# One tile for the last 64 query rows of both heads of a pair, in causal attention ahead of two MLPs

## The chip, the cores and the metric

The kernel runs on one core of a Trainium2 chip. The metric is the device time of one execution in microseconds (us). Five engines work side by side, each through its own queue in order: PE (TensorE, matrix products; PEld are its weight loads), DVE (VectorE), ACT (ScalarE), POOL (GpSimd) and SP (which only issues DMAs).

## What is computed

The reference, cut to what matters (B = 2 batches, H = 8 heads, S = 576 positions, D = 64):

```python
scores = q @ k.T / sqrt(D)                       # per batch and head, 576 x 576
bias = -(cum[:, None] - cum[None, :])            # cum: running sum of max(s, 0)
scores = where(causal, -1e9, scores + minimum(bias, 0))
attn = softmax(scores)                           # each query row over its keys
x = (attn @ v) -> [1152 tokens, 512]
x = leaky_relu(x @ w_in) @ w_out                 # d_ff 2048
out = sum over 4 experts e of p[:, e] * (relu(x @ w1[e]) @ w2[e])   # F 1024
```

576 is four and a half tiles of 128 query rows. All is float32; the two weights of the first MLP arrive as 64-bit floats and are converted on the chip.

## The kernel before

**Attention.** The work is cut into 16 units. A unit is one batch, one pair of heads and one part of the query rows: units 0 to 7 take rows 0 to 255 (tiles 0 and 1), units 8 to 15 rows 256 to 575 (tiles 2, 3 and 4). Tile 4 has only 64 rows left, so it is laid over rows 448 to 575 (`tiles` holds `min(i * P, S - P)`): its first 64 rows are tile 3's last once more, and what is computed for them is overwritten. A unit of the second kind has six items, tile 4, 3, 2 for head 0 and 1 each: (4,0), (4,1), (3,0), (3,1), (2,0), (2,1).

Each item goes through steps that lag behind each other, by the table `STEPS`: in iteration i of the loop the program writes the scores of item i, the exponentials of item i-1, the transposes of item i-3, the products with values of item i-5 and `finish` of item i-7.

- `scores`: in a unit of the second kind, q and k are split into a high and a low part; two products (`ks,qs` and `kd,qs`) go into the PSUM tile `ps_sc`. One DVE instruction (shown as CUSTOM_DVE_ANT_0) adds the mask, scales, writes `z` and keeps the row's minimum `mn`. Tile 4 has 576 keys and goes in two pieces, 448 and 128.
- `exps`: ACT turns `z` into the exponentials.
- `transposes`: PE turns each 128 x 128 block of `z` (five for tile 4) into `ps_pt`, ACT copies that to `pv`.
- `values`: PE multiplies each block of `pv` (the stationary operand) with 65 columns of `vs` (a column of ones for the row sums, and 64 of v) into `ps_o`. These are plain float32 products: each stands as two instructions, so tile 4 shows as x10 for one head. After the last item of a unit DVE divides (`st`, `xo`).
- `finish`: three transposes of `xo` into `ps_x`, and one ACT copy to `x`.

**What is woven in.** Between the steps, at two of the three `yield`s of an iteration, the program advances `main`, the first MLP for the first 512 tokens (`ps_u`, `ps_d`: three or so 512-column products a step). `WOVEN * KD / (2.0 * (48 - 6))` sets how many steps per `yield`: 72 over 84, 0.857. At two of three it also advances `units_of_w` (`supply`: the conversion of the 64-bit weights, 16 blocks `r`, mostly DVE work of 1024 columns into `raw`, which then go to DRAM as `w_f`) and `late` (weight blocks loaded back from `w_f`). `split_keys` prepares the keys and queries of the next unit (`qs`, `ks`) in four calls, one per iteration, from the unit's first item on; the last DVE operation of it, the second `ks<-kr,ks`, stands in the fourth item's iteration.

Up to the end of the attention every engine keeps the order in which the program is written (`keep_in_program_order`). The loop's first part ends at iteration 39; while there is little of `main` to weave, it puts small products on `idle` there. When the attention is done, DVE and POOL prepare the second half of the first MLP (`t`, `sums`, `w`), which PE begins when the first half's `ps_d` are done. The queues of DMAs: SP issues the loads of q, k, v (`qr`, `kr`, `vs`) and the loads from `w_f`, POOL the load `kd<-in_k_dram`, ACT the 64-bit weights.

Of the kernel before, what the change touches and what calls it, by code (L numbers as in the profile page):

```python
# [19 lines left out]
def attention_moe_moe2(ctx: ExitStack, tc: tile.TileContext, q, k, v, s, w_in, w_out, probs, w1, w2, out):  # L20
# [34 lines left out]
    P = 128  # L55
# [469 lines left out]
    mask = ap.tile([P, S], F32, name="mask", bufs=1)  # L525

# [53 lines left out]
    q_s = [ap.tile([P, 2, 2, S // 2 + 32], F32R, tag=f"q{i}", name="qs", bufs=1) for i in range(2)]  # L580
    q_e, k_e = [], []

    def pads(pool):
# [15 lines left out]
        ones = pool.tile([P, 2, S // 2 + 32], F32, name="ones")  # L599
        nc.gpsimd.memset(ones[D:DK], 1.0)  # L600
        return ones
# [10 lines left out]
    def load_keys(n, queue=None):  # L612
# [9 lines left out]
        else:  # L622
            qr = ap.tile([P, 2, S // 2 + 32], F32, tag="qr", name="qr")
            for j in range(2):
                nc.sync.dma_start(qr[j * D : (j + 1) * D], q_of)
# [14 lines left out]
    def split_keys(n):  # L640
# [7 lines left out]
        nc.scalar.copy(qs[:, 0], qr)  # L648
        yield
        nc.vector.tensor_tensor(qs[:D, 1], qr[:D], f32(qs[:D, 0]), ALU.subtract)  # L650
# [16 lines left out]
    class Unit:  # L667
# [3 lines left out]
        def __init__(self, n):  # L671
            b, hp, i0, i1 = self.of = of_unit(n)
            self.items = [(i, j) for i in reversed(range(i0, i1)) for j in range(2)]
# [5 lines left out]
        def scores(self, i, j):  # L679
# [6 lines left out]
            own = slice(a - tiles[i0][0], kw - tiles[i0][0])  # L686
            for pc, keys in enumerate([slice(0, kw)] if kw <= 512 else [slice(0, a), slice(a, kw)]):
# [6 lines left out]
                nc.vector.tensor_tensor_reduce(  # L694
                    out=z[:, keys], in0=ps, in1=mask[:, S - kw + keys.start : S - kw + keys.stop], scale=-(D ** -0.5),
# [18 lines left out]
        def values(self, i, j):  # L714
# [3 lines left out]
            pv, cols = self.pv.pop((i, j)), slice(j * (D + 1), (j + 1) * (D + 1))  # L718
# [11 lines left out]
        def finish(self, i, j):  # L730
# [5 lines left out]
            base, q0, q1 = tiles[i0][:2] + tiles[i1 - 1][2:]  # L736
            x = ps_t.tile([P, 512], F32, tag="pt", name="ps_x")[:, : q1 - base]
            for i in reversed(range(i0, i1)):
                nc.tensor.transpose(x[:, tiles[i][0] - base : tiles[i][2] - base], self.xo[:, i - i0].rearrange("p h c -> p (h c)"), ident)
# [5 lines left out]
            else:  # L745
                nc.scalar.copy(x_t[1][:, hp, dst], x)
# [187 lines left out]
```

## Time and profile before

| | |
|---|---|
| median of 3 timed runs | 726.08 us (724.13, 726.08, 728.84) |
| span of the profiled execution | 724.3 us, first to last instruction; no other time of that execution is given |
| PE busy | 708.1 us, 98% of the span |
| DVE, ACT, POOL busy | 442.5, 322.8, 253.1 us |
| units 8 to 15 (first score to the end of the last transposes) | 51.8 to about 209 us |

The profiled execution lies within the three timed ones. In the rows below nearly every instruction stands on line 43, since one helper issues them all; they are told apart by the tile names. A matmul row's time is from its start to its modelled end, and those overlap: what a chain of products costs is read from the start of its first to the start of what follows it on PE.

### The profile page before, as it was taken

Reading aid. Unit: us, or ns where it says so; the run is one execution under the profiler, and the core shown is the slowest. Engines: PE = TensorE matmul, PEld = TensorE weight load, DVE = VectorE, ACT = ScalarE, POOL = GpSimd, SP = SyncE. Lnnn points to the kernel's source line nnn. Section 1 sums busy time; section 2 is a strip of 40 time slices with the busy share of each in tenths; the row PEclk is TensorE's granted clock in tenths of the full one; section 3 lists DMA queues with packets and bytes.
Section 4 is the critical chain, followed back from the end, with each engine's and each line's share of the span. In section 5 each row is a group of like instructions: output and inputs, shape, how many; then the busy total and the mean of one; then the engine's idle time right before and its main releaser. Section 6 shows DMA issues by size and latency. Waiting matters only on the chain.

```text
span 724.3 us, 11414 instructions
## 1 busy us (share of the span) xinstructions
PE 708.1 (98%) x4376; PEld 645.2 (89%) x4376; DVE 442.5 (61%) x901; ACT 322.8 (45%) x650; POOL 253.1 (35%) x226
## 2 busy tenths in 40 slices
PE   7889999999999999999999999999999999999998
PEld 7779889888878999999988989989889898898996
DVE  5878797998769656844953644545436354364452
ACT  4767877876645755534432322314224133232220
POOL 5000000000018788883362442704625227142200
PEclk9999999999999999999999999999999999999999
DMA  8876867585452232221120202102102011020002
GB/s 217 228 194 176 217 181 240 184 246 181 176 203 88 76 99 89 63 84 59 33 85 1 88 29 59 59 1 59 58 30 59 30 60 59 0 59 1 1 30 101
DMA packets 41878, 70.68 MB, mean 98 GB/s; under 512 B 4112, under 2 KB 23328, under 8 KB 41824
## 3 DMA queue, kind: packets, MB, share of 16 engines
q1 hardware_dynamic: 31296, 41.87, 20.0%
q10 hardware_dynamic: 9376, 25.73, 10.9%
q0 software_dynamic: 1152, 2.36, 1.6%
q8 instruction: 34, 0.56, 0.3%
q14 instruction: 20, 0.16, 0.1%
HBM read 59.11 MB, written 10.82 MB: 97 GB/s over the span
## 4 chain that ended last, share of the span: by engine, by line
PE 89%; DMA 3%; DVE 3%; ACT 2%; issue 1%; POOL 1%; ACTq 0%; DVEq 0%; POOLq 0%; SPq 0%
PE ps_d L43 40%; PE ps_u L43 36%; PE ps_o L43 5%; PE ps_sc L43 4%; PE ps_pt L43 3%; DMA raw<-w_f 1%; DMA cum_d<-cum 1%; DMA ke<-cum 1%; DVE t L43 1%; ACT z L43 1%; ACT w L43 1%; DVE w L43 0%; ACT pv L43 0%; DVE z L43 0%; DMA w_f<-raw 0%
## 5 line engine op out<-in xcount | busy, mean ns | idle before, releaser
L43 PE MATMUL ps_u<-t,w 128*128 128x320 f32 (+1 forms) x1680 | 236.5, 299 | 1.2 <-DVE t L43 1.2
L43 PEld LDWEIGHTS ps_u<-t,w 128*128 128x128 f32 x1680 | 233.0, 189 | 4.8 <-DVE t L43 1.4
L43 PE MATMUL ps_d<-w,ht 128*128 128x512 f32 (+1 forms) x876 | 203.4, 388 | 0.0
L43 PEld LDWEIGHTS ps_d<-w,ht 128*128 128x128 f32 x876 | 161.0, 188 | 31.5
L43 POOL TENSOR_TENSOR w<-raw,w 128x512 fp32r<-128x512 f32 (+2 forms) x72 | 108.5, 1527 | 219.1 <-ACT w L43 219.1
L43 ACT ACTIVATE ht<-ps_u 128x320 fp32r<-128x320 f32 (+2 forms) x176 | 74.3, 433 | 161.6 <-DVE ps_u L43 129.1
L43 DVE SCALAR_TENSOR_TENSOR oacc<-ps_d,pn,oacc 128x512 f32<-128x512 f32 (+1 forms) x64 | 47.5, 743 | 104.0 <-PE ps_d L43 104.0
L43 PE MATMUL ps_d<-ht,w 128*128 128x320 f32 (+1 forms) x576 | 109.6, 340 | 1.0 <-DVE y L43 1.0
L43 ACT CAST w<-raw 128x512 fp32r<-128x512 f32 (+2 forms) x96 | 64.6, 710 | 82.5 <-PE ps_d L43 76.0
L43 PEld LDWEIGHTS ps_d<-ht,w 128*128 128x128 f32 x576 | 90.9, 188 | 7.0 <-ACT t L43 1.4
L43 DVE SCALAR_TENSOR_TENSOR ht<-ps_u,ht 128x320 fp32r<-128x320 f32 (+1 forms) x128 | 56.4, 453 | 23.3 <-ACT ht L43 22.0
L43 PEld LDWEIGHTS ps_o<-vs,pv 128*128 128x128 f32 x480 | 63.0, 191 | 8.5 <-issue 4.0
L43 DVE TENSOR_TENSOR ps_u<-ps_u,tmp 128x320 f32<-128x320 f32 (+1 forms) x120 | 56.2, 471 | 23.3 <-PE ps_u L43 21.7
L43 PE MATMUL ps_o<-vs,pv 128*128 128x65 f32 x480 | 62.9, 267 | 2.9 <-issue 1.3
L43 DVE TENSOR_TENSOR tmp<-ps_u,tmp 128x320 f32<-128x320 f32 (+1 forms) x80 | 36.9, 464 | 40.2 <-PE ps_u L43 39.3
L43 POOL TENSOR_TENSOR w<-sums,w 128x1024 fp32r<-128x1024 f32 x24 | 58.6, 2443 | 7.5 <-ACT w L43 7.5
L43 POOL TENSOR_TENSOR sums<-raw 128x256 f32<-128x256 f32 x48 | 38.1, 812 | 59.3 <-DMA raw<-w_f 57.8
L43 PE MATMUL ps_u<-x,w 128*128 128x512 f32 x192 | 56.7, 411 | 0.9 <-DVE x L43 0.9
L43 ACT ACTIVATE z<-z,mn 128x256 f32<-128x256 f32 (+4 forms) x80 | 48.5, 607 | 20.2 <-DVE mn L43 16.7
L43 POOL DMA_DIRECT2D kd<-in_k_dram x8 | 5.1, 639 | 141.4 <-PE ps_sc L43 141.4
L43 DVE CUSTOM_DVE_ANT_0 z<-ps_sc,mask 128x256 f32<-128x256 f32 (+4 forms) x80 | 41.0, 513 | 15.4 <-PE ps_sc L43 13.8
L43 ACT COPY pv<-ps_pt 128x512 f32<-128x512 f32 (+3 forms) x96 | 38.9, 422 | 13.0 <-PE ps_pt L43 12.4
(77 smaller groups left out, 659.2 us busy)
## 6 DMA issues: line engine op xcount, KB each, us to landing
raw<-in_moe_w_dram SPq DMA_DIRECT2D x32, 512.0 KB, 3.6
raw<-w_f SPq DMA_DIRECT2D x24, 512.0 KB, 4.0
r<-in_moe_w_in_dram ACTq DMA_DIRECT2D x8, 1024.0 KB, 6.6
w_f<-raw ACTq DMA_DIRECT2D x16, 512.0 KB, 4.1
r<-in_moe_w_out_dram ACTq DMA_DIRECT2D x8, 1024.0 KB, 7.9
qr<-in_q_dram SPq DMA_DIRECT2D x16, 160.0 KB, 7.3
kd<-in_k_dram POOLq DMA_DIRECT2D x8, 288.0 KB, 7.5
kr<-in_k_dram SPq DMA_DIRECT2D x8, 288.0 KB, 3.7
```

Source lines behind the costliest of these rows:

```text
L43: ins = call(*args, **kw)
```

## The change

The 64 last rows of the two heads of a pair become one tile of 128 rows, head 0 in rows 0 to 63, head 1 in rows 64 to 127. Its item is (4, None); a unit of the second kind has five items in place of six, 72 instead of 80 in all. For the scores, `qs` gets 64 columns of zeros and head 1's last 64 rows are put ahead of its others, so that a window of 128 columns holds [last rows of head 0, zeros] and another [zeros, last rows of head 1]; four products (two of each head) are summed in one `ps_sc`. A mask of its own, `mask2`, serves the last 128 keys. There is then one minimum, one exponential, one set of five transposes, and the products with values take both heads' 130 columns at once. `finish` copies the result in three pieces. `qr` is loaded in six DMAs in place of two. The weaving's numbers are set to 40 items in place of 48, and `units_of_w` gets one more step in every third iteration.

```diff
+    mask2 = ap.tile([P, P], F32, name="mask2", bufs=1)
...
+    LAST = S - (QT - 1) * P
+    QC = S - half[0]
+    q_s = [ap.tile([P, 2, 2, QC + LAST], F32R, tag=f"q{i}", name="qs", bufs=1) for i in range(2)]
...
+        for x in q_s:
+            nc.gpsimd.memset(f32(x[:, :, 0, QC:]), 0.0)
+        own = mask2[:, P - LAST :]
+        nc.gpsimd.memset(mask2, 0.0)
+        nc.gpsimd.affine_select(own, own, [[-1, LAST]], ALU.is_ge, MASKED, -D, 1)
+        nc.gpsimd.memset(own[:D], 0.0)
+        nc.gpsimd.affine_select(own[:D], own[:D], [[-1, LAST]], ALU.is_ge, MASKED, 0, 1)
...
-            for j in range(2):
-                nc.sync.dma_start(qr[j * D : (j + 1) * D], q_of)
+            for part in (slice(0, D), slice(D, P)):
+                nc.sync.dma_start(qr[part, 0], q_of[:, 0])
+                nc.sync.dma_start(qr[part, 1, LAST:], q_of[:, 1, : QC - LAST])
+                nc.sync.dma_start(qr[part, 1, :LAST], q_of[:, 1, QC - LAST :])
...
-            self.items = [(i, j) for i in reversed(range(i0, i1)) for j in range(2)]
+            self.items = [(i, j) for i in reversed(range(i0, i1)) for j in (range(2) if i < QT - 1 else (None,))]
...
+                qs = self.qs.rearrange("p l j c -> p l (j c)")
+                at_q = i * P - tiles[i0][1] + (QC + 2 * LAST) * (j or 0)
+                heads, at_q = ((0, 1), (QC - LAST, QC)) if j is None else ((j,), (at_q,))
...
-                    nc.tensor.matmul(ps, self.qs[:, 0, j, own], self.ks[:, j, keys], start=True, stop=False)
-                    nc.tensor.matmul(ps, self.qs[:DK, 1, j, own], self.kd[:DK, j, keys], start=False, stop=True)
+                    for h, c in zip(heads, at_q):
+                        nc.tensor.matmul(ps, qs[:, 0, c : c + P], self.ks[:, h, keys], start=(h == heads[0]), stop=False)
+                        nc.tensor.matmul(ps, qs[:DK, 1, c : c + P], self.kd[:DK, h, keys], start=False, stop=(h == heads[-1]))
...
-            pv, cols = self.pv.pop((i, j)), slice(j * (D + 1), (j + 1) * (D + 1))
+            pv = self.pv.pop((i, j))
+            cols = slice(0, 2 * D + 2) if j is None else slice(j * (D + 1), (j + 1) * (D + 1))
...
-                nc.scalar.copy(x_t[1][:, hp, dst], x)
+                full = QC - LAST
+                nc.scalar.copy(x_t[1][:, hp, dst.start : dst.start + full], x[:, :full])
+                for j, part in enumerate((slice(0, D), slice(D, P))):
+                    nc.scalar.copy(x_t[1][part, hp, dst.start + full : dst.stop], x[part, full + j * LAST : full + (j + 1) * LAST])
...
-                owed += WOVEN * KD / (2.0 * (48 - 6))
+                owed += WOVEN * KD / (2.0 * (40 - 6))
...
-            if at_ % 3 != 1 and not ending:
+            if (at_ % 3 != 1 or i % 3 == 0) and not ending:
                 next(units_of_w, None)
```

On PE, the start of a unit in the middle of the stretch (here `ps_pt x4` and the `ps_o` ahead of `ps_x` belong to items of the unit before). Before, the two scores of tile 4 and, five items on, their values:

```order
L43 MATMUL ps_sc<-ks,qs 128x448
L43 MATMUL ps_sc<-kd,qs 128x448
L43 MATMUL ps_sc<-ks,qs 128x128
L43 MATMUL ps_sc<-kd,qs 128x128
L43 MATMUL ps_d<-ht,w 128x512 x3
L43 MATMUL ps_pt<-ident,z 128x128 x4
L43 MATMUL ps_o<-vs,pv 128x65 x5
L43 MATMUL ps_x<-ident,xo 128x128 x3
L43 MATMUL ps_sc<-ks,qs 128x448
L43 MATMUL ps_sc<-kd,qs 128x448
L43 MATMUL ps_sc<-ks,qs 128x128
L43 MATMUL ps_sc<-kd,qs 128x128
```

And after, at the start of a unit:

```order
L43 MATMUL ps_sc<-ks,qs 128x448
L43 MATMUL ps_sc<-kd,qs 128x448
L43 MATMUL ps_sc<-ks,qs 128x448
L43 MATMUL ps_sc<-kd,qs 128x448
L43 MATMUL ps_sc<-ks,qs 128x128
L43 MATMUL ps_sc<-kd,qs 128x128
L43 MATMUL ps_sc<-ks,qs 128x128
L43 MATMUL ps_sc<-kd,qs 128x128
L43 MATMUL ps_d<-ht,w 128x512 x3
L43 MATMUL ps_pt<-ident,z 128x128 x4
L43 MATMUL ps_d<-ht,w 128x512 x3
L43 MATMUL ps_o<-vs,pv 128x130 x5
```

The eight score products of tile 4 stand together now, and the products with values have 130 columns, five in place of two times five. (These rows count a plain float32 product once, where the profile counts its two instructions.) Over the whole program PE has 40 transposes fewer (200 for 240) and 40 products with values fewer (160 of 65 and 40 of 130 columns for 240 of 65).

On DVE, from the last operation that prepares the next unit's keys (`ks<-kr,ks`) to the first score of that unit (`z`, 448 columns). Before:

```order
L43 TENSOR_TENSOR ks<-kr,ks 64x576
L43 TENSOR_SCALAR raw<-raw 128x1024
L43 ISA z,mn<-ps_sc,mask 128x384
L43 ISA mn 128x1
L43 TENSOR_TENSOR ht<-ps_u,ht 128x512
L43 TENSOR_SCALAR st<-ps_o 128x6
L43 RECIPROCAL st<-st 128x6
L43 TENSOR_TENSOR xo<-ps_o,st 128x384
L43 TENSOR_SCALAR raw<-raw 128x1024
L43 ISA z,mn<-ps_sc,mask 128x384
L43 ISA mn 128x1
```

And after:

```order
L43 TENSOR_TENSOR ks<-kr,ks 64x576
L43 TENSOR_TENSOR w<-raw,w 128x1024
L43 ISA z,mn<-ps_sc,mask 128x384
L43 ISA mn 128x1
L43 TENSOR_SCALAR raw<-raw 128x1024
L43 TENSOR_SCALAR st<-ps_o 128x6
L43 RECIPROCAL st<-st 128x6
L43 TENSOR_TENSOR xo<-ps_o,st 128x384
L43 TENSOR_SCALAR raw<-raw 128x1024
L43 ISA z,mn<-ps_sc,mask 128x448
```

One item's scores (384 columns) stand between the prepared keys and the unit that uses them, where two stood.

On DVE, from the last unit's division (`xo`) to the first `y` behind it. Before:

```order
L43 TENSOR_TENSOR xo<-ps_o,st 128x384
L43 TENSOR_TENSOR ht<-ps_u,ht 128x512
L43 TENSOR_TENSOR w<-raw,w 128x512 x2
```

And after:

```order
L43 TENSOR_TENSOR xo<-ps_o,st 128x384
L43 TENSOR_SCALAR raw<-raw 128x1024
L43 TENSOR_TENSOR ht<-ps_u,ht 128x512
L43 SCALAR_TENSOR_TENSOR raw<-r_2219,raw 128x1024 x2
L43 TENSOR_TENSOR w<-raw,w 128x512 x2
```

Three operations of the last block's conversion have moved behind the end of the attention. Elsewhere the order has two loads from `w_f` fewer (22 for 24), and POOL six short operations more ahead of its first `kd` load. Behind the attention the operations and their order are the same but for a few places.

## Rows read from the trace of the kernel before

**Rows 1.** The page's part 1: busy us, share of the span and instructions of each engine.

```profile
PE 708.1 (98%) x4376; PEld 645.2 (89%) x4376; DVE 442.5 (61%) x901; ACT 322.8 (45%) x650; POOL 253.1 (35%) x226
```

**Rows 2.** Windows of three units: length, busy us of each engine, clock, DMA share, GB/s.

```profile
102.70:120.86 18.16, 18.16 (x123) 16.25 (x123) 16.08 (x33) 13.92 (x24) 0.58 (x1) 1.00 0.76 207
120.86:139.24 18.38, 18.38 (x124) 16.18 (x123) 15.42 (x33) 13.87 (x26) 0.58 (x1) 1.00 0.84 265
139.24:157.38 18.14, 18.14 (x124) 16.27 (x123) 16.03 (x33) 15.32 (x28) 0.58 (x1) 1.00 0.57 186
```

**Rows 3.** Timeline of PE: start, us to the modelled end, instructions, idle before.

```profile
92.24 0.48 PE L43 MATMUL ps_sc<-ks,qs 128*128 128x512 f32 x1
...
104.60 1.22 PE L43 MATMUL ps_o<-vs,pv 128*128 128x65 f32 x10
105.66 0.50 PE L43 MATMUL ps_x<-ident,xo 128*128 128x128 f32 x3
...
113.48 0.71 PE L43 MATMUL ps_pt<-ident,z 128*128 128x128 f32 x5
114.02 0.78 PE L43 MATMUL ps_o<-vs,pv 128*128 128x65 f32 x6
...
115.75 0.71 PE L43 MATMUL ps_pt<-ident,z 128*128 128x128 f32 x5
116.21 0.94 PE L43 MATMUL ps_d<-ht,w 128*128 128x512 f32 x3
...
148.72 0.47 PE L43 MATMUL ps_sc<-ks,qs 128*128 128x512 f32 x1
...
157.38 0.45 PE L43 MATMUL ps_sc<-ks,qs 128*128 128x448 f32 x1
```

**Rows 4.** Timeline of PE earlier: unit 7's first score; float32 products on `idle`.

```profile
44.60 0.65 PE L43 MATMUL ps_sc<-ke,qe 128*128 128x256 f32 x2
...
66.42 0.39 PE L43 MATMUL ps_u<-idle 128*128 128x128 f32 x2
66.65 1.23 PE L43 MATMUL ps_o<-vs,pv 128*128 128x65 f32 x10
```

**Rows 5.** Timeline of DVE: last `ks` operations of two units; tile 4's score pieces.

```profile
97.48 0.75 DVE L43 TENSOR_TENSOR ks<-kr,ks 64x576 fp32r<-64x576 f32 x1
...
104.36 0.62 DVE L43 CUSTOM_DVE_ANT_0 z<-ps_sc,mask 128x448 f32<-128x448 f32 x1
...
105.14 0.35 DVE L43 CUSTOM_DVE_ANT_0 z<-ps_sc,mask,mn 128x128 f32<-128x128 f32 x1
...
151.73 0.75 DVE L43 TENSOR_TENSOR ks<-kr,ks 64x576 fp32r<-64x576 f32 x1
```

**Rows 6.** Timeline of all engines at the end of the attention.

```profile
204.51 1.22 DVE L43 SCALAR_TENSOR_TENSOR raw<-r,raw 128x1024 uint32<-128x1024 uint32 x1
...
207.31 0.56 DVE L43 TENSOR_TENSOR xo<-ps_o,st 128x384 f32<-128x384 f32 x1
...
212.39 8.44 PE L43 MATMUL ps_d<-ht,w 128*128 128x512 f32 x36 [0.99 <-DVE y L43]
...
237.09 8.08 PE L43 MATMUL ps_u<-t,w 128*128 128x320 f32 x54
...
238.16 1.47 DVE L43 TENSOR_TENSOR t<-sums,t 128x1280 fp32r<-128x1280 f32 x1
```

**Rows 7.** Groups of instructions: busy us, mean ns of one, idle before.

```profile
L43 DVE TENSOR_SCALAR raw<-raw 128x1024 f32<-128x1024 f32 (+1 forms) x32 | 22.0, 689 | 0.4
...
L43 ACT COPY x<-ps_x 128x320 f32<-128x320 f32 x8 | 3.4, 427 | 5.9 <-PE ps_x L43 5.9
```

**Rows 8.** Timeline of SP, which issues the loads, from unit 8's queries to unit 7's decay.

```profile
30.45 1.28 SPq L43 DMA_DIRECT2D qr<-in_q_dram  x2
...
34.43 0.63 SPq L43 DMA_DIRECT2D ke<-cum  x1
```

**Rows 9.** Timeline of POOL: its first two loads of keys.

```profile
9.72 1.33 POOL L43 DMA_DIRECT2D kd<-in_k_dram  x2
```

More of the change, by code (lines that the diff above doesn't have):

```diff
@@ L579, in attention_moe_moe2 @@
     DK = D + 2
-    q_s = [ap.tile([P, 2, 2, S // 2 + 32], F32R, tag=f"q{i}", name="qs", bufs=1) for i in range(2)]
+    LAST = S - (QT - 1) * P
+    QC = S - half[0]
+    q_s = [ap.tile([P, 2, 2, QC + LAST], F32R, tag=f"q{i}", name="qs", bufs=1) for i in range(2)]
     q_e, k_e = [], []
@@ L598, in pads @@
                 nc.gpsimd.memset(x[: P - S % P, QT - 1], 0.0)
-        ones = pool.tile([P, 2, S // 2 + 32], F32, name="ones")
+        ones = pool.tile([P, 2, QC], F32, name="ones")
         nc.gpsimd.memset(ones[D:DK], 1.0)
+        for x in q_s:
[5 more added lines that the diff above has]
+        nc.gpsimd.affine_select(own[:D], own[:D], [[-1, LAST]], ALU.is_ge, MASKED, 0, 1)
         return ones
@@ L647, in split_keys @@
         nc.gpsimd.dma_start(kd[:D], k[b, 2 * hp : 2 * hp + 2].rearrange("h d s -> d h s"))
-        nc.scalar.copy(qs[:, 0], qr)
+        nc.scalar.copy(qs[:, 0, :, :QC], qr)
         yield
-        nc.vector.tensor_tensor(qs[:D, 1], qr[:D], f32(qs[:D, 0]), ALU.subtract)
+        nc.vector.tensor_tensor(qs[:D, 1, :, :QC], qr[:D], f32(qs[:D, 0, :, :QC]), ALU.subtract)
         for j in range(2):
@@ L686, in scores @@
             own = slice(a - tiles[i0][0], kw - tiles[i0][0])
+            heads = (j,)
+            if self.ks is not None:
+                qs = self.qs.rearrange("p l j c -> p l (j c)")
+                at_q = i * P - tiles[i0][1] + (QC + 2 * LAST) * (j or 0)
+                heads, at_q = ((0, 1), (QC - LAST, QC)) if j is None else ((j,), (at_q,))
             for pc, keys in enumerate([slice(0, kw)] if kw <= 512 else [slice(0, a), slice(a, kw)]):
@@ L691, in scores @@
                 else:
-                    nc.tensor.matmul(ps, self.qs[:, 0, j, own], self.ks[:, j, keys], start=True, stop=False)
-                    nc.tensor.matmul(ps, self.qs[:DK, 1, j, own], self.kd[:DK, j, keys], start=False, stop=True)
+                    for h, c in zip(heads, at_q):
+                        nc.tensor.matmul(ps, qs[:, 0, c : c + P], self.ks[:, h, keys], start=(h == heads[0]), stop=False)
+                        nc.tensor.matmul(ps, qs[:DK, 1, c : c + P], self.kd[:DK, h, keys], start=False, stop=(h == heads[-1]))
                 nc.vector.tensor_tensor_reduce(
-                    out=z[:, keys], in0=ps, in1=mask[:, S - kw + keys.start : S - kw + keys.stop], scale=-(D ** -0.5),
+                    out=z[:, keys], in0=ps, in1=mask2 if pc else mask[:, S - kw + keys.start : S - kw + keys.stop], scale=-(D ** -0.5),
                     scalar=3.0e38 if pc == 0 else mn[:, 0:1], op0=ALU.add, op1=ALU.min, accum_out=mn[:, pc : pc + 1],
@@ L735, in finish @@
                 return
-            base, q0, q1 = tiles[i0][:2] + tiles[i1 - 1][2:]
-            x = ps_t.tile([P, 512], F32, tag="pt", name="ps_x")[:, : q1 - base]
+            x = ps_t.tile([P, 512], F32, tag="pt", name="ps_x")[:, : (i1 - i0) * P]
             for i in reversed(range(i0, i1)):
-                nc.tensor.transpose(x[:, tiles[i][0] - base : tiles[i][2] - base], self.xo[:, i - i0].rearrange("p h c -> p (h c)"), ident)
+                nc.tensor.transpose(x[:, (i - i0) * P : (i - i0 + 1) * P], self.xo[:, i - i0].rearrange("p h c -> p (h c)"), ident)
             c = int(i0 > 0)
@@ L824, in attention_moe_moe2 @@
                 if at_ % 3 == 0 and i in (6, 8):
-                    nc.scalar.copy(q_s[i // 2 - 3][D:DK, 1], ones[D:DK])
+                    nc.scalar.copy(q_s[i // 2 - 3][D:DK, 1, :, :QC], ones[D:DK])
                 if at_ % 3 == 1:
```

2 lines of the change are left out of this document (1 added, 1 removed).

## The prediction, made before the changed kernel ran

> **What bounds the kernel now.** I read the page's busy shares first. PE is busy for 708.1 of 724.3 us [rows 1]. A busy PE is not by itself a bound, since the ends of its products are modelled, so I went to the stretch that the change touches, units 8 to 15, and cut it at the first score of each unit. In three units in the middle PE shows no idle time at all and runs at its upper clock, 1.00 or 2.4 GHz; DVE is busy for 15.4 to 16.1 us of some 18.2, or 87%, and ACT for 13.9 to 15.3 [rows 2]. The timeline of PE in one of these units then shows chain after chain without a gap between them, each starting where the one before has been streamed. So what a chain costs is the distance from its first start to the start of what follows, and what PE need no longer do there comes off the end, as long as DVE, ACT and the loads keep up. The three windows are 18.16, 18.38 and 18.14 us long, 18.23 in the mean: that is the price of a unit of six items [rows 2].
>
> **What the change takes from PE.** Each of eight units loses one set of five transposes. Such a set takes 114.02 - 113.48 = 0.54 us, and another 116.21 - 115.75 = 0.46 [rows 3]; I take 0.50. That is saved whole.
>
> The products with values go from two chains of ten instructions with 65 columns to one of ten with 130. A chain with 65 columns takes 105.66 - 104.60 = 1.06 us, 0.106 an instruction [rows 3], so the two take 2.12. No row has a plain float32 product of 130 columns. Its price lies between 0.106 (the columns hide behind the load of the 128 x 128 weights) and 0.212 (nothing hides, double the columns cost double). The nearest row is that of float32 products of 128 columns, with weights of the same size: two instructions take 66.65 - 66.42 = 0.23 us, 0.115 each [rows 4]. I take that: 10 x 0.115 = 1.15 us, and 2.12 - 1.15 = 0.97 saved, with bounds of 0 and 1.06.
>
> A rule speaks against this. The Trainium skill, "TensorE: Matmul & The Clock Gate", section "The mechanism" of Part 3, says that weight loads overlap products in flight only when these use other row groups of the array. All 128 rows are used here, so by that rule load and product would follow one another and the added columns would be paid in full. The trace doesn't bear it out: 128 columns, each instruction with a load of its own, take 0.009 us more than 65 [rows 3, 4]. What the sum would be by it is the second rival.
>
> The scores cost the same: eight products of the same columns, moved together; I put 0 there, and a few hundredths either way from one switch fewer. So a unit loses 0.50 + 0.97 = 1.47 us of PE, and eight units 11.8; by the bounds of the values, 4.0 to 12.5.
>
> **What it takes from and adds to the others.** DVE loses one pair of score pieces a unit, 0.62 + 0.35 us [rows 5], about 1.0. Its share in a unit would go from 15.84 of 18.23 us to 14.84 of 16.76, 87% to 89%: still under PE. ACT loses an exponential and two copies, and in `finish` has three copies for one of 0.43 us [rows 7]; with a busy share of 79% before it is no bound, and I put 0 there. The woven numbers give a unit 10.6 steps of `main` for 10.3, and 11.7 steps of the conversion for 12, so no engine's load per unit changes beyond this; a step of `main` that is done earlier is not done later.
>
> SP issues six `qr` loads for two. Two took 1.28 us, so four more may take 2.6, and everything behind them on SP is later by that once for each unit. The tightest place I find is unit 7: its decay `ke<-cum` is issued at 34.43, behind the `qr` of unit 8 [rows 8], and its scores start at 44.60 [rows 4]. Ten microseconds hide 2.6. I cost it at nothing; without that cover it would be 2.6 us once. POOL has six short operations more ahead of its first `kd` loads at 9.72 [rows 9], whose data are used from 51.8 us on: nothing, too.
>
> **Where some of it may be given back.** First, the keys of the next unit. Their last operation on DVE stands in the fourth item's iteration, and the next unit's scores came three items later: 157.38 - 148.72 = 8.66 us [rows 3]. It ended 97.48 + 0.75 - 92.24 = 5.99 us after that item's scores in the unit where it was latest, and 151.73 + 0.75 - 148.72 = 3.76 where it was earliest [rows 3, 5], the six units in between. With five items only two remain, 2/5 of 16.76 us, or 6.7. That leaves 0.7 to 2.9 us: enough if DVE's lag stays as it is, and nothing to spare in the worst unit. I allow 1 us for all seven units together; the bounds are 0 and, if DVE's lag grows by one operation of 1.22 us [rows 6] in the tight ones, some 4.
>
> Second, the end of the attention. The last block of the conversion now ends behind the last division: one operation of 0.69 us [rows 7] and two of 1.22 [rows 6], 3.1 us that DVE does between `xo` and the `y` for which PE already waits 0.99 us at 212.39 [rows 6]. Part of it fits into gaps in which DVE waits for ACT there. I allow 1 us, bounds 0 and 3.1. The start of the second half at 237.09, where DVE's last `t` ends only at 239.6 [rows 6], keeps its order and moves with the rest; 0.
>
> **The sum.** 724.3 - 11.8 + 1 + 1 = 714.5 us for the profiled execution. The median of the runs before, 726.08, is 1.8 above that execution's span, so the median forecast is 716.3; I say 716.
>
> **The rivals.**
> First, all of it arrives and more: the keys are never late, and PE's idle time of a few tenths per unit at the scores and divisions shrinks with the lighter load on DVE and ACT. Then 726.1 - 12.5 - 0.5 = 713. For it speaks that the lags of the steps, counted in items, become longer in time, about 3.35 us an item for 3.04. Against it: DVE's share rises.
>
> Second, the products with 130 columns hide nothing and cost 0.212 each. Then only the transposes are saved, 4.0 us, and the time is 722. Row 4's products of 128 columns speak against it, with the one doubt that they are pairs and not chains of ten.
>
> Third, the gain is real but half of it goes to waits: 0.6 us a unit at the keys in seven units, and the full 3.1 at the end of the attention, 7.3 together: 726.1 - 11.8 + 7.3 = 721.6. For it speaks DVE's 89%, in one queue in order, in which operations of 1.22 us stand ahead of short ones; against it, that PE showed no idle time with 87%.
>
> Fourth, slower than before: DVE falls behind so far that each new unit waits for its keys. The place is the first score of units 9 to 15. It decides from the point where the wait eats the gain: 11.8 / 7 = 1.7 us a unit, so a lag of 6.7 + 1.7 = 8.4 us where the largest seen is 6.0. With a lag of 9.5 the waits are 7 x 2.8 = 19.6 us, and the time is 734. For it speaks only that the cover falls from 8.7 to 6.7 us; against it, that the demand on DVE per unit falls as well.
>
> **How the numbers follow.** I give my forecast (714 to 719) 0.72, the first rival 0.08, the second 0.07, the third 0.09, the fourth 0.04. A change of 1%, 7.3 us, is about what runs that spread over 724.1 to 728.8 can tell from none; faster by that means under 718.8. Nearly all of the forecast and the first rival lie there: 0.82. The second and third lie within 1%: 0.14. Slower: 0.04. A range of 712.5 to 721.5 leaves out the second and the fourth rival and about half of the third, 0.16, and a little below.
>
> **What the profile after would show.** Right: 40 products of 130 columns (x80 in the trace), a chain of ten from first start to the next chain in 1.1 to 1.2 us; units of 16.6 to 17 us with PE idle near 0; the second half of the MLP beginning 9 to 12 us before 237.09; the rest of the span as long as before. Wrong in the second rival's way: that chain in 2 us or more. In the third's and fourth's: idle time of PE before `ps_sc` put down to DVE's `ks`, or a longer wait for `y` at the end of the attention. What would make the forecast wrong beyond these is a wait that no row of before shows, such as three copies of ACT holding `ps_x` when the next transposes want the bank.

## The result, and the profile after

The changed kernel takes 719.5 us (median of 10 runs, 717.1 to 722.7) where the kernel before takes 726.05 (10 runs): a ratio of 0.990, 95% interval 0.988 to 0.993. It is 6.5 us faster; 716 were forecast, inside a range of 712.5 to 721.5. The profiled execution took 717.48, its span is 715.7, 1.8 less, as the prediction had assumed.

The page's part 1 (busy us, share of the span and instructions of each engine), which answers to [rows 1]:

```profile
PE 696.9 (97%) x4256; PEld 633.2 (88%) x4256; DVE 433.7 (61%) x867; ACT 315.1 (44%) x640; POOL 253.9 (35%) x232
```

PE has lost 11.2 us of busy time and 120 instructions, DVE 8.8 us, about what the prediction took off them. Three units in the middle, as windows from first score to first score, answer to [rows 2] (length, busy us of PE, PEld, DVE, ACT and POOL, granted clock, DMA share, GB/s):

```profile
111.07:128.24 17.17, 17.17 (x112) 15.27 (x111) 13.14 (x26) 11.27 (x23) 0.58 (x1) 1.00 0.88 239
128.24:145.21 16.97, 16.70 (x109) 14.61 (x108) 15.61 (x29) 15.17 (x28) 0.58 (x1) 1.00 0.73 231
145.21:162.75 17.54, 17.44 (x111) 15.17 (x111) 16.36 (x31) 12.85 (x23) 0.00 (x0) 1.00 0.36 104
```

They are 17.23 us long in the mean where they were 18.23, and they hold 33, 30 and 33 products of `main` where each held 30. Those two more a unit, at 0.23 us, are the 0.46 us between 17.23 and the 16.76 of the prediction. The merged tile's products with values, on PE's timeline (start, us to the modelled end), with the chain that follows; they answer to the x10 chains of [rows 3]:

```profile
131.40 1.28 PE L43 MATMUL ps_o<-vs,pv 128*128 128x130 f32 x10
132.43 0.48 PE L43 MATMUL ps_sc<-ks,qs 128*128 128x512 f32 x1
```

From start to start these ten take 1.03 us, 0.103 an instruction: 130 columns cost no more than 65 (1.06 in [rows 3]). So the products were saved as forecast, and a little more. The loss is further on, at the end of the attention, which answers to [rows 6]. PE there, from the last transposes to the second half of the MLP (in brackets PE's wait before a row, and what ended it):

```profile
195.96 0.49 PE L43 MATMUL ps_x<-ident,xo 128*128 128x128 f32 x3
196.21 3.68 PE L43 MATMUL ps_d<-ht,w 128*128 128x512 f32 x15
201.76 5.71 PE L43 MATMUL ps_d<-ht,w 128*128 128x512 f32 x24 [1.88 <-DVE y L43]
207.31 5.60 PE L43 MATMUL ps_u<-x,w 128*128 128x512 f32 x24
...
218.25 10.29 PE L43 MATMUL ps_d<-ht,w 128*128 128x512 f32 x37 [2.79 <-DVE ht L43]
228.38 0.90 PE L43 MATMUL ps_u<-t,w 128*128 128x320 f32 x5
```

PE waits 4.67 us where it waited 0.99 before [rows 6]. What it waits for stands on ACT and DVE in the same stretch. ACT (ACTq is its queue issuing a DMA):

```profile
198.32 0.34 ACTq L43 DMA_DIRECT2D w_f<-raw  x1
198.70 0.69 ACT L43 COPY x<-ps_x 128x256 f32<-128x256 f32 x3 [1.02 <-DVE raw L43]
...
207.38 1.66 ACT L43 CAST w<-raw 128x512 fp32r<-128x512 f32 x3 [7.24 <-DMA raw<-w_f]
...
212.94 1.26 ACT L43 CAST t<-sums 128x1280 fp32r<-128x1280 f32 x1
```

And DVE:

```profile
193.97 0.56 DVE L43 TENSOR_TENSOR xo<-ps_o,st 128x384 f32<-128x384 f32 x1
...
195.81 2.48 DVE L43 SCALAR_TENSOR_TENSOR raw<-r,raw 128x1024 uint32<-128x1024 uint32 x2
...
199.41 0.68 DVE L43 TENSOR_TENSOR y<-ps_d,y 128x512 f32<-128x512 f32 x1
...
214.23 3.37 DVE L43 TENSOR_TENSOR t<-sums,t 128x1280 fp32r<-128x1280 f32 x1 [2.15 <-ACT t L43]
217.52 0.68 DVE L43 TENSOR_TENSOR ht<-ps_u,ht 128x512 fp32r<-128x512 f32 x1
```

Read the two together. DVE finishes the last converted block at 198.3, behind `xo`; from 193 to 202.4 us it has no gap, so its own work delays `y`. ACT stands at the store of that block until then, with the copies of `ps_x` behind it. The block goes to DRAM, SP issues the next loads from `w_f` only at 201.08, and ACT, in order, stands 7.24 us at a cast that waits for such a load, with its other casts behind it. Not all of that wait is new. In the kernel before ACT also stands at these casts, 2.04 us for such a load and 4.72 for PE's `ps_d`:

```profile
213.49 0.62 ACT L43 CAST w<-raw 128x512 fp32r<-128x512 f32 x1 [2.04 <-DMA raw<-w_f]
...
219.50 1.14 ACT L43 CAST w<-raw 128x512 fp32r<-128x512 f32 x2 [4.72 <-PE ps_d L43]
```

In the changed kernel `t` is then cast at 212.94. DVE stands 2.15 us for it and does its own `t` in 3.37 us; the `ht` that frees PE is queued behind. In the kernel before, the answering `t` took 1.48 us. POOL is at work beside it in both kernels; what differs is which of the two engines began first. After (POOL), and then before (DVE and POOL):

```profile
213.86 2.39 POOL L43 TENSOR_TENSOR w<-sums,w 128x1024 fp32r<-128x1024 f32 x1
```

```profile
226.44 1.48 DVE L43 TENSOR_TENSOR t<-sums,t 128x1280 fp32r<-128x1280 f32 x1
226.47 2.04 POOL L43 TENSOR_TENSOR sums<-raw 128x256 f32<-128x256 f32 x1
```

After, `t` begins within POOL's `w<-sums,w` and ends 1.35 us behind its end (217.60 and 216.25). Before, `t` begins 0.03 us ahead of POOL's `sums`, and it is POOL's operation that is long, 2.04 us where another of the same shape, at 214.07, took 0.74.

PE's last wait costs more than its 2.79 us. Windows from its start on, with the columns of [rows 2]:

```profile
215.46:218.25 2.79, 0.00 (x0) 0.00 (x1) 2.79 (x3) 0.55 (x2) 2.64 (x2) 1.00 0.52 146
218.25:220.16 1.91, 1.91 (x5) 1.52 (x6) 1.88 (x4) 0.00 (x0) 1.90 (x3) 0.53 0.11 3
220.16:222.00 1.84, 1.84 (x6) 1.41 (x5) 1.42 (x3) 0.84 (x1) 1.84 (x2) 0.56 0.02 5
222.00:224.00 2.00, 2.00 (x10) 1.66 (x9) 0.87 (x2) 2.00 (x4) 2.00 (x3) 1.00 0.00 0
```

PE's granted clock is 0.53 and 0.56 behind the wait, near 1.2 GHz, for 3.75 us: five and six products where 2 us hold ten at 1.00.

One stretch of PE's timeline measures all this in every kernel: from the first score of unit 8 to the first `ps_u<-t`, which begins the second half of the MLP. Behind it before and after are alike (724.3 - 237.09 = 487.2 us and 715.7 - 228.38 = 487.3; 487.2 to 489.0 in all the traces). What lies ahead of unit 8 differs more: it begins at 50.0 to 56.5 us. In the kernel before the stretch is 237.09 - 51.81 = 185.28 us, after it is 228.38 - 50.01 = 178.37. The prediction's sum (11.8 saved, 2 given back) makes 175.5.

### The profile page after: what moved, and what is told of

Read it like the earlier page. It is cut to its first block, busy times and chain, and to the rows that moved or that the text cites. A ratio compares the mean times of both kernels' runs of the same rounds, so it can differ in the third digit from the quotient of the medians.

```text
span 715.7 us, 11167 instructions
## 1 busy us (share of the span) xinstructions
PE 696.9 (97%) x4256; PEld 633.2 (88%) x4256; DVE 433.7 (61%) x867; ACT 315.1 (44%) x640; POOL 253.9 (35%) x232
## 4 chain that ended last, share of the span: by engine, by line
PE 82%; DVE 7%; DMA 4%; ACT 2%; POOL 2%; issue 1%; SPq 0%; ACTq 0%; POOLq 0%; DVEq 0%
PE ps_d L43 39%; PE ps_u L43 34%; PE ps_o L43 4%; PE ps_sc L43 3%; PE ps_pt L43 2%; DVE raw L43 2%; DMA qe<-in_q_dram 1%; DVE t L43 1%; ACT w L43 1%; DVE z L43 1%; DMA vs<-in_v_dram 1%; DMA raw<-w_f 1%; DMA ke<-in_k_dram 1%; DVE w L43 1%; POOL sums L43 1%
## 5 line engine op out<-in xcount | busy, mean ns | idle before, releaser
L43 PEld LDWEIGHTS ps_o<-vs,pv 128*128 128x128 f32 x400 | 53.5, 191 | 6.8 <-issue 2.3
L43 PE MATMUL ps_o<-vs,pv 128*128 128x65 f32 (+1 forms) x400 | 53.3, 267 | 2.1 <-DVE xo L43 1.2
L43 ACT ACTIVATE z<-z,mn 128x256 f32<-128x256 f32 (+4 forms) x72 | 42.4, 588 | 12.0 <-DVE mn L43 7.2
L43 DVE CUSTOM_DVE_ANT_0 z<-ps_sc,mask 128x256 f32<-128x256 f32 (+4 forms) x72 | 36.0, 501 | 12.5 <-PE ps_sc L43 9.7
L43 ACT COPY pv<-ps_pt 128x512 f32<-128x512 f32 (+3 forms) x80 | 33.2, 424 | 21.2 <-PE ps_pt L43 20.7
```

The costliest lines, as they stand in the source:

```text
L43: ins = call(*args, **kw)
```

## The theories, and what the runs gave

Theory T: the miss is the late last block of the conversion. It holds DVE 3.1 us, but above all ACT, and by `t`, `y` and `ht` it makes PE wait. Rival R1: behind the attention there are six products of `main` fewer, since the new weaving number does more of it earlier. PE then has less to do while `y` and `ht` are made: the waits are missing cover, whatever the conversion does. Rival R2: DVE and POOL slow each other at the start of the second half in any case. Two more runs put the saved work of PE back, part by part.

Medians in us, the ratio to the kernel before (726.0 to 726.4 in these comparisons) with its 95% interval, and of each profiled execution: the stretch, PE's waits in it ahead of the last `ps_x` (units) and from there on (end), summed over its timeline.

| kernel | median | ratio | stretch | units | end |
|---|---|---|---|---|---|
| before | 726.1 | | 185.28 | 2.76 | 0.99 |
| changed | 719.5 | 0.990 (0.988-0.993) | 178.37 | 3.44 | 4.67 |
| changed, once more | 719.1 | 0.990 (0.987-0.993) | 179.25 | 4.11 | 4.65 |
| conversion early in all units | 719.6 | 0.991 (0.987-0.995) | 177.02 | 4.81 | 2.29 |
| before, conversion late | 729.6 | 1.005 (1.002-1.008) | 185.95 | 1.55 | 3.30 |
| values as two sets of 65 | 726.2 | 0.999 (0.996-1.002) | 183.63 | 2.00 | 3.28 |
| conversion early at the end | 716.9 | 0.986 (0.983-0.989) | 174.41 | 3.66 | 2.28 |
| conversion only at the end | 716.9 | 0.987 (0.983-0.990) | 173.51 | 3.38 | 2.29 |
| weaving at 48 | 728.4 | 1.003 (1.000-1.005) | 186.90 | 6.11 | 8.32 |
| transposes twice | 721.2 | 0.993 (0.990-0.995) | 178.07 | 1.22 | 4.36 |
| early at the end, weaving at 41 | 713.9 | 0.982 (0.980-0.984) | 173.94 | 4.09 | 1.97 |
| late, weaving at 41 | 718.7 | 0.990 (0.987-0.992) | 179.20 | 4.59 | 4.21 |
| early at the end, weaving at 48 | 730.1 | 1.005 (1.003-1.008) | 192.24 | 7.93 | 5.62 |
| weaving at 48, store on SP | 725.8 | 0.999 (0.996-1.001) | 183.97 | 6.25 | 5.19 |

## The experiments

**The changed kernel once more**, as a base on the same chip.

> The changed kernel once more, beside the others on one chip. Every theory: 719.5 us within the spread of its runs (717 to 723), ratio to the kernel before 0.990; the profile again has PE waits of some 2 and 3 us for DVE's `y` and `ht` behind the attention.

719.1 us; the waits behind the attention are there again, 1.87 and 2.78. But this time the clock holds behind them, and falls elsewhere. PE's timeline in the middle units:

```profile
111.94 0.88 PE L43 MATMUL ps_pt<-ident,z 128*128 128x128 f32 x4 [1.53 <-ACT pv L43]
```

And the window behind that wait:

```profile
111.94:116.01 4.07, 4.07 (x16) 3.70 (x17) 2.42 (x7) 2.71 (x6) 0.00 (x0) 0.58 1.04 289
```

A wait of 1.53 us for ACT's copy to `pv` is followed by 4.07 us at a granted clock of 0.58.

**The conversion early in all units.** The changed kernel, with one number in the line that advances the conversion:

```diff
-            if (at_ % 3 != 1 or i % 3 == 0) and not ending:
+            if (at_ % 3 != 1 or i % 2 == 0) and not ending:
```

> The changed kernel with one difference: the conversion of the weights is advanced at the third yield in every second iteration in place of every third, so that its last block is done before the last `xo`, as it was in the kernel before. Theory T (the late last conversion delays its store and reload, and with them ACT's queue, `t` and `ht`): the PE waits for `y` and `ht` behind the attention go from 4.7 us together back to about 1, and the time falls 3 to 5 us, to 715 to 716. Rival R1 (fewer steps of `main` are left as cover behind the attention, whatever the conversion does): unchanged, 719 to 720. Rival R2 (DVE and POOL collide on `t` at the start of the second half in any case): unchanged, with `t` again at 3.4 us.

719.6 us: by the time alone, T has failed. The waits at the end did fall, from 4.67 to 2.29. What took their place is in the groups of PE (out<-in, count, busy us, mean ns, idle before and what ended it), first this kernel's scores:

```profile
L43 PE MATMUL ps_sc<-ks,qs 128*128 128x448 f32 (+3 forms) x64 | 25.1, 398 | 3.1 <-DVE mn L43 3.1
```

In the changed kernel the same group shows:

```profile
L43 PE MATMUL ps_sc<-ks,qs 128*128 128x448 f32 (+3 forms) x64 | 24.7, 393 | 0.4 <-DVE mn L43 0.3
```

2.8 us more of waits for the minima. They stand in three places (0.95, 1.31 and 0.88 us), and in the last two DVE has an operation of the conversion ahead of the minimum. Behind the one of 1.31 us PE's granted clock is 0.54 and 0.60 in the next two windows of 2 us. The two changes of the waits are about as large: the block's lateness seems to cost, and so does work that DVE is given in the middle units. The runs below take them apart.

**The kernel before with the conversion late.** It is the reverse test: in the kernel before, the conversion is skipped once in ten iterations, so that its last block falls behind the last `xo`; the weaving stays.

```diff
-            if at_ % 3 != 1 and not ending:
+            if at_ % 3 != 1 and not ending and (at_ % 3 or i % 10):
```

> The kernel before with one difference: the conversion is skipped once in ten iterations, so that its last block (one operation of 0.69 and two of 1.2 us on DVE) falls behind the last `xo`, as in the changed kernel. Theory T: it loses what the change lost there, 3 to 5 us: 729 to 731, with ACT blocked for several us by the reload of that block and PE waiting for `y` and `ht`. R1: nothing, 726, since as many steps of `main` are left as before. R2: nothing, 726.

729.6 us, 3.3 more than before, and the interval of the ratio, 1.002 to 1.008, leaves out 1. PE behind the attention, which stands against 0.99 in [rows 6]:

```profile
212.41 8.42 PE L43 MATMUL ps_d<-ht,w 128*128 128x512 f32 x36 [2.14 <-DVE y L43]
...
229.93 8.69 PE L43 MATMUL ps_d<-ht,w 128*128 128x512 f32 x37 [1.16 <-DVE ht L43]
```

The late block alone makes the first wait longer and brings the second into a kernel that has neither the merged tile nor less cover. R1 and R2 said nothing would change. That it costs 3.3 us rests on the medians: in the one trace the waits at the end are 2.3 us more and those in the units 1.2 less than in the kernel before, and the stretch is only 0.67 longer. PE's clock is 1.00 behind both waits in that trace; over the twelve executions its mean is 0.996, where the kernel before has 0.998.

**Values as two sets of 65 columns.** It puts the ten instructions a unit back that the change took away:

```diff
-            for kt in range(i + 1):
-                nc.tensor.matmul(self.o[:, i - i0, cols], ...)
+            for cols in (cols,) if j is not None else (slice(0, D + 1), slice(D + 1, 2 * D + 2)):
+                for kt in range(i + 1):
+                    nc.tensor.matmul(self.o[:, i - i0, cols], ...)
```

> The changed kernel with one difference: the merged tile's products with values are made as two sets of 65 columns in place of one of 130, ten instructions of 0.10 us more a unit. If a product of 130 columns costs no more than one of 65, as the trace of the changed kernel says: 8 x 1.03 = 8.2 us slower than the changed kernel, 727 to 728, units 1.0 us longer. If the columns were paid for elsewhere (the two theories on the price differ here): less than half of it, under 723.5.

726.2 us, 7.1 more than the changed kernel beside it. The chain in its trace:

```profile
140.74 2.34 PE L43 MATMUL ps_o<-vs,pv 128*128 128x65 f32 x20
142.88 0.47 PE L43 MATMUL ps_sc<-ks,qs 128*128 128x512 f32 x1
```

Twenty take 2.14 us where ten of 130 columns take 1.03. So the merged products are worth 8 x 1.11 = 8.9 us of PE, and most of it, 7.1, shows in the median. The traces' stretches show 4.4 to 5.3. The waits in the units are 1.4 us lower than in the changed kernel and so are those at the end: some of the added work lies in the former, while the edit does not explain the latter.

**Transposes twice.** The merged tile's five transposes are made a second time over the same place:

```diff
-                for kt in range(k0, k1):
+                for kt in (*range(k0, k1), *(range(k0, k1) if j is None else ())):
```

> The changed kernel with the merged tile's five transposes made twice (the second set writes the same values over the first). If such a set costs PE 0.50 us and nothing hides it: 8 x 0.50 = 4.0 us slower than the changed kernel, 723 to 724. If part of what the change saved there was idle time that PE had anyway: less than 2 us.

721.2 us: 2.0 more, half of the 4.0. The intervals of the two kernels overlap, and the stretches of their traces are alike (178.07 and 178.37, the latter with its 3.75 us at a low clock), so neither nothing nor the whole 4.0 is ruled out. The group of transposes in this kernel and, behind the next sentence, in the changed one shows where part of it may have gone.

```profile
L43 PE MATMUL ps_pt<-ident,z 128*128 128x128 f32 x240 | 38.8, 275 | 2.1 <-ACT pv L43 1.5 <-DVE x L43 0.5
```

Without the second set PE waits 1.5 us more there, 1.1 of it for ACT's copies to `pv`:

```profile
L43 PE MATMUL ps_pt<-ident,z 128*128 128x128 f32 x200 | 34.5, 275 | 3.6 <-ACT pv L43 2.6 <-DVE x L43 0.9
```

All waits in the units are 1.22 us with the second set and 3.44 without. So a unit that is lighter on PE spends part of what it is given in waits for ACT and DVE.

**The conversion early at the end.** Up to iteration 65 the order is the changed kernel's; from there on every yield advances the conversion, so that its last operation stands ahead of the last division. The added steps fall into the last unit and the iterations behind it, where DVE has no keys of a next unit to prepare and, in the end, no scores:

```diff
-            if (at_ % 3 != 1 or i % 3 == 0) and not ending:
+            if (at_ % 3 != 1 or i % 3 == 0 or i >= 66) and not ending:
```

> The changed kernel up to the items of the last unit; from iteration 66 on the conversion is advanced at every yield, so that its last block is done two operations of the last division earlier, and the units in the middle keep their order. The run before this one brought the last block forward in all units, took 2.4 us of waits away behind the attention, and paid 2.8 us more before the scores, for DVE's `mn`. Theory T, refined (the late block costs 2.4 us, and DVE has no room for it in the middle units): the waits for `y` and `ht` fall to about 2.3 us, the waits for `mn` stay at 0.3, and the time falls by 2 to 3 us, to 716.5 to 717.5. Rival (the block costs nothing that its place decides, what is left at the end is cover): 719 to 720.

716.9 us. PE behind the attention, the rows that answer to those of the changed kernel:

```profile
200.83 5.72 PE L43 MATMUL ps_d<-ht,w 128*128 128x512 f32 x24 [0.87 <-DVE y L43]
...
215.89 6.42 PE L43 MATMUL ps_d<-ht,w 128*128 128x512 f32 x27 [1.41 <-DVE ht L43]
```

Half of the waits are gone, those for `mn` stay at 0.3, and from 40 to 240 us no window of 2 us shows a clock under 0.98. This is what T, refined, said. DVE's `t`, in 2.63 us, again ends 1.35 us behind POOL's `w<-sums,w`, which here ends 1.5 us earlier, counted from the start of the eleven `ps_d` ahead of PE's wait.

**The conversion only at the end.** As that, without the extra step every third iteration (`at_ % 3 != 1 or i >= 60`).

> The changed kernel with no extra step of the conversion before iteration 60 (two yields in three, as in the kernel before), and all yields from there on, so that the last block is done before the last `xo`. Theory T, refined: DVE is lighter in the middle units and the last block is early: as the run above or a few tenths better, 716 to 717.5, with no waits for `mn` over 0.3. Rival (DVE's operations that wait for room in the last units now delay `xo` and the keys there): waits before `ps_o` or `ps_sc` in the last two units, 719 or more.

716.9 us again, with the same 0.88 and 1.41 at the end. The waits for `mn` rose to 1.7, against what was expected; it is one wait, and DVE has an operation of the conversion ahead of that minimum. Those for `pv` fell from 1.48 to 0.40, and the units' waits together are 3.38.

**More cover, late conversion.** The changed kernel with the weaving's number left at 48, so that 39 products of `ps_u` and 48 of `ps_d` stand behind the attention:

```diff
-                owed += WOVEN * KD / (2.0 * (40 - 6))
+                owed += WOVEN * KD / (2.0 * (48 - 6))
```

> The changed kernel with the weaving's number for `main` left at 48 items: 72 steps over 84 yields in place of 68, so that fewer steps are done within the attention and some 39 products of `ps_u` more stand behind it; the conversion is as late as in the changed kernel. R1 (what is missing behind the attention is cover): the waits for `y` and `ht` go to about 1 us and the time to 716. Theory T (the late block stops ACT and with it `t` and `ht`): what PE does first behind the attention is `ps_u`, which needs no `y`, so the 1.9 us before `y` may go, while the 2.8 us for `ht` stay unless they are covered by the longer stretch: 717 to 719.

728.4 us, 9 more, which neither theory had. PE behind the attention:

```profile
201.07 7.56 PE L43 MATMUL ps_u<-x,w 128*128 128x512 f32 x24 [7.25 <-DVE ht L43]
```

ACT ahead of it, and then the windows of the wait and of the 24 products behind it:

```profile
193.95 0.34 ACTq L43 DMA_DIRECT2D w_f<-raw  x1
194.62 0.69 ACT L43 COPY x<-ps_x 128x256 f32<-128x256 f32 x3 [6.08 <-DVE raw L43]
```

```profile
193.82:201.07 7.25, 0.00 (x0) 0.03 (x1) 4.70 (x8) 3.80 (x9) 3.27 (x4) 0.80 0.52 182
201.07:208.47 7.40, 7.40 (x24) 5.92 (x25) 2.07 (x5) 2.53 (x5) 0.00 (x0) 0.73 0.14 54
```

More products are no cover if they are the wrong ones: a row of `ps_u` needs ACT and DVE to take its results out, and ACT stood 6.08 us at the store of the late block. The next two runs ask how much of this is the block's.

**The same with the conversion early at the end** (the edit above, and 48).

> The kernel with the weaving's number at 48, that took 728.4 and in which PE waited 7.25 us for `ht` behind the attention, with the conversion brought forward at the end. If that wait is the late block's (ACT stands at the store of the block, until DVE has converted it, with the copies that free `ps_u` behind it): it goes, and the time is 717 to 719. If it is the weaving's number that costs (PE outruns ACT and DVE with 24 and more `ps_u` in a row): 725 or more.

730.1 us: T's forecast for this kernel fell. The wait went from 7.25 to 4.00 only,

```profile
204.16 8.58 PE L43 MATMUL ps_u<-x,w 128*128 128x512 f32 x24 [4.00 <-DVE ht L43]
```

and the units' waits rose to 7.93, of which 7.01 are for `pv`. With 48 the weaving's number is a cost of its own, in the units and at the end. Part of it is PE's clock: the mean granted clock is 0.989 over the twelve executions of each of these two kernels with 48, where the changed kernel beside the others has 0.996. The difference of 0.007 would be some 5 us of 728, an estimate that takes the time to go with the clock; the two are 9 and 11 us slower.

**The same with the late conversion, and the last block's store issued by SP.** One instruction moves from ACT's queue to SP's:

```diff
-            nc.scalar.dma_start(w_f32[stream[n][2]], raw)
+            (nc.sync if n == CONVERTED - 1 else nc.scalar).dma_start(w_f32[stream[n][2]], raw)
```

> The kernel with the weaving's number at 48 and the late conversion (728.4), with one instruction moved: the store of the last converted block is issued by SP in place of ACT; no other queue changes. If what costs is ACT standing at that store (6.1 us in the trace, with the copies of `ps_u` and `x` behind it): most of the 7.25 us go, 720 to 723. If it is the block's late data themselves (DVE's work, the reload): 726 to 728.5.

725.8 us, 2.6 less; the intervals of the two ratios touch. ACT's copy behind the attention waits for PE now:

```profile
192.42 0.69 ACT L43 COPY x<-ps_x 128x256 f32<-128x256 f32 x3 [1.89 <-PE ps_x L43]
```

And PE's wait is half as long:

```profile
199.40 7.30 PE L43 MATMUL ps_u<-x,w 128*128 128x512 f32 x24 [3.58 <-DVE ht L43]
```

So ACT standing at that store was worth 3.7 us of PE's wait in this kernel. The time fell by less than the 5 to 8 us that were expected. What is left of the wait is about what it is with the early block (4.00).

**Cover as before, late conversion.** The number 41 gives a unit 72/70 x 10 = 10.29 steps of `main`, what the kernel before gives it (72/84 x 12), and leaves as many products around the last `ps_x`.

> The changed kernel (conversion late) with the weaving's number at 41: 6 products more behind the last `ps_x`, as in the kernel before. R1: the waits behind the attention fall from 4.7 to about 1 to 2 us and the time to 716 to 717. Theory T: the late block holds ACT as before, the waits stay at 3 to 5 us, and the time at 718.5 to 720.

718.7 us, the changed kernel's time within the intervals: cover alone brings nothing. PE's wait is now in one piece:

```profile
204.21 11.04 PE L43 MATMUL ps_d<-ht,w 128*128 128x512 f32 x36 [4.21 <-DVE y L43]
```

ACT stands at the store ahead of it, until DVE has converted the block:

```profile
200.80 0.69 ACT L43 COPY x<-ps_x 128x256 f32<-128x256 f32 x3 [2.92 <-DVE raw L43]
```

And the window behind PE's wait has a clock of 0.74:

```profile
204.21:215.08 10.87, 10.87 (x36) 8.74 (x37) 4.54 (x7) 2.44 (x6) 5.96 (x6) 0.74 0.51 191
```

**Cover as before, conversion early at the end.** Both edits together.

> The kernel of the run with the conversion early at the end (716.9), with the weaving's number at 41 items in place of 40: as many products of `main` (3 and 45 of `ps_d`) stand around the last `ps_x` as in the kernel before, 6 more behind it than at 40. R1 in what is left of the waits (0.9 before `y`, 1.4 before `ht`): the 1.4 us go, and the time is 715 to 716. If the waits that are left have another cause: 717, and the wait for `ht` stays at 1.4.

713.9 us, 12.5 less than before and 4.8 less than the run above, from which only the place of the conversion differs; the two intervals are apart. It is the fastest version here. PE behind the attention:

```profile
199.91 8.44 PE L43 MATMUL ps_d<-ht,w 128*128 128x512 f32 x36 [1.39 <-DVE y L43]
208.19 5.60 PE L43 MATMUL ps_u<-x,w 128*128 128x512 f32 x24
213.63 11.16 PE L43 MATMUL ps_d<-ht,w 128*128 128x512 f32 x48
224.62 12.49 PE L43 MATMUL ps_u<-t,w 128*128 128x320 f32 x84
```

The window that answers to the one of the run above:

```profile
199.91:208.19 8.28, 8.28 (x37) 6.83 (x38) 5.33 (x7) 2.05 (x6) 5.20 (x6) 1.00 0.41 135
```

The wait for `ht` is gone, as R1 had it for what was left, though the one for `y` grew from 0.87 to 1.39 and 0.58 for `xo` came in ahead of the last `ps_x`. From the 36 products of `ps_d` to the first `ps_u<-t` it takes 224.62 - 199.91 = 24.71 us, the kernel before 237.09 - 212.39 = 24.70 [rows 6]: the end is the old one again, and the stretch is 11.3 us shorter.

What follows. The late block costs 4.8 us at 41, 3.3 in the kernel before, and 2.2 to 2.6 at 40, where the intervals still touch but two versions gave the same; it is the main cause of the miss of 3.5. Of the 2.4 us of waits that it adds at 40, by the traces 1.0 is the wait for `y`, DVE's own time, and 1.4 the wait for `ht`, which goes by the store, the load, ACT and POOL; no run takes these four apart at 40. R1 alone is refuted (718.7), but it adds to T: with the block early, the six products seem to be worth something more. How much is open: the medians of 40 and 41 differ by 3.0 us with intervals that overlap, the two traces by 0.5 in the stretch. R2 is half right. DVE and POOL do meet without the late block: with the block early at 40, DVE's `t` takes 2.63 us and PE still waits 1.41 for `ht`. In the kernel before and in the fastest one it is DVE's two `w<-raw,w` that meet `w<-sums,w`, 4.04 us for 1.29 elsewhere, and PE has enough to do meanwhile.

## Why the prediction was right, and where it was not

It held in its direction and range; 3.5 us are missing to the forecast of 716. The 719.5 lies outside the 714 to 719 to which 0.72 was given, and above the 718.8 that was called the limit of faster, with 0.82 below it (0.02 more than the forecast and the first rival hold together). The interval of the ratio, up to 0.993, tells it from no change all the same. Some of the fit is luck: by the stretch, 1.0 us came from chains that were cheaper than priced and 1.0 from an allowance that was not needed, against 2.7 more of waits at the end than allowed, 0.7 in the units and, as an estimate, 1.7 by the clock.

- **What PE need no longer do** (11.8 us): right. The products with values came out a little better than priced, 1.03 us a chain for 1.15; the price that I took was above the true one, the lower bound of 0.106 an instruction was nearest. The fastest kernel shows the term with the end and the weaving of the kernel before: 11.3 us of the stretch, in which PE waits 2.3 us more.
- **DVE, ACT, SP and POOL at nothing**: right for SP and POOL, nearly so for the other two. The waits in the units rose by 0.7 to 1.4 us, the most of it for ACT's copies to `pv`, which the prediction had put at 0.
- **The keys of the next unit** (allowance 1 us): nothing. In no run's stretch is a wait of PE put down to `ks`. In the changed kernel the last `ks` is ready 1.3 to 3.7 us ahead of the next unit's first score (161.43 and 162.75 in the tightest place). The smallest lag in the kernel before was 3.57 us, in unit 8 (57.79 to 61.36), not 3.76; nothing hangs on it.
- **The end of the attention** (allowance 1 us, bounds 0 and 3.1): this is the step that failed. It was the right place, and the three operations were seen, but they were priced as DVE's own time. That is 1.0 us of PE's added waits, just what was allowed. The runs show what else hangs on them: the store, the loads behind it, and the copies and casts that stand behind these in ACT's queue and that POOL, DVE and then PE need. With the clock it is worth 2.2 to 2.6 us of the time in the changed kernel and up to 4.8 by the weaving that it meets, where 1 was allowed and 3.1 was the bound.
- **"A step of `main` that is done earlier is not done later"**, put at 0: true of the work, not of the cover. The six products that moved ahead no longer stood behind the last division; by the traces that is 0.5 us, by the medians 3.0 with intervals that overlap, where the block is early, and nothing where it is late.
- **A cost that no term had**: PE's clock behind its new waits. The mean granted clock is 0.9957 over the 12 executions beside the other kernels, where the kernel before has 0.9979 over 29; 0.0022 of 720 us are 1.6, an estimate, and part of it is in the 2.2 to 4.8 above.
- **The rivals.** The second (130 columns hide nothing) fell with the chain of 1.03 us. The rule of the Trainium skill behind it ("TensorE: Matmul & The Clock Gate", section "The mechanism"), as the prediction put it, does not describe these chains: all 128 rows are in use in each, and the added columns are hidden. The same section also names the load into a background weight buffer as a case that overlaps; no run here shows whether that is what happens. The third (half the gain goes to waits) came nearer in its time, 721.6, than the forecast, and was right in one of its two places: the end of the attention, not the keys.

Of what the profile after was to show, the chain came out at 1.03 us for 1.1 to 1.2, the units at 17.2 for 16.6 to 17 (with two products of `main` more in each), and the second half of the MLP began 8.7 us earlier for 9 to 12, 1.8 of which came ahead of unit 8; the rest of the span is as long as before.

## What to carry to other kernels

A step that slips past the end of a phase is to be priced by its whole chain: follow its result through store, reload and the queue of each engine that handles it, and name what is queued in order behind each of these waits; here 3.1 us of DVE became up to 4.8 us of the whole. When items get fewer, the rates tied to them (here two weaving numbers) are part of the change: try first with the work per unit and what is left for the end as they were. For the weaving of `main` what that is worth stays open here (nothing with the late block, up to 3.0 us with the early one). Background work goes where its engine has room (here the last unit, behind which no keys and scores are waiting), not evenly: the same conversion made early in all units brought nothing in six runs.

## What the runs showed of the hardware

In chains of ten, a plain float32 instruction with 128 x 128 weights costs 0.103 us with 130 columns and 0.106 with 65 (0.107 in the twenty of the run with two sets): at these two sizes the columns are free, and instructions are what counts.

PE's granted clock fell from the upper of its two levels toward the lower one (1.2 GHz) behind some waits of 1.31 to 7.25 us, and such a wait then cost more than itself. It fell to 0.53 behind 2.79 us of waiting (1.7 us beyond the wait, an estimate from the 3.75 us at 0.53 and 0.56), stayed at 1.00 behind 2.78 us in another execution of the same kernel, fell to 0.58 behind 1.53 and to 0.54 behind 1.31, and stayed at 1.00 behind 1.39 in the fastest kernel. The 36 products of `ps_d` took 10.87 us at 0.74, behind 4.21 us of waiting, and 8.28 at 1.00. What decides which it is, the runs do not show.

DVE's `t<-sums` (128x1280) took 1.48 us where it began 0.03 us ahead of an operation of POOL, which was then long, and 3.37 and 2.63 us where it began within POOL's `w<-sums,w`; in both it ended 1.35 us behind that. The Trainium skill, "SBUF — State Buffer", section "SBUF: two separate sides", has DVE and GpSimd lock one pair of ports against each other when DVE reads two inputs from SBUF and the GpSimd operation reads SBUF: the one that starts first holds the pair for its whole instruction. These rows agree with that; no run here takes POOL's work away.
